# Halving the relu blocks, scoring three bursts ahead and accumulating in open PSUM banks in a fused attention and MoE kernel

## The chip, the cores and the metric

The kernel runs on one core of a Trainium2 chip. The metric is the device time of one execution in microseconds (us), as the median of several executions on the same chip. Times are compared only with runs of the kernel before that were taken in the same rounds on the same chip.

## The reference, cut to what matters

```python
B, N, m, C = (4, 12544, 32, 128)          # x: B x N x C, inducing: m x C
def mab(q, kv):                            # attention with one head
    s = scale * (q @ kv.transpose(0, 2, 1))
    s = s - s.max(-1, keepdims=True)
    a = np.exp(s)
    a /= a.sum(-1, keepdims=True) + 1e-09
    return a @ kv
h = mab(I, x)                              # phase 1: 32 inducing points look at a batch's 12544 tokens
attn_out = mab(x, h)                       # phase 2: every token looks at the 32 rows of h
# MoE, d_ff = 1024
h1 = x @ w1 ; h2 = x @ w2                  # x is attn_out now
out = np.maximum(h1, h2) @ w_out
```

The kernel uses max(a, b) = b' + relu(a - b), folds h into the weights (hwd = h times (w2 - w1), m1 = h times w1 times w_out), and never forms attn_out. What is left per 128 tokens in phase 2 is: relu of (hwd with e2), then w_out, plus the m1 part, divided by the softmax's sum.

## The kernel before

A batch has 98 columns of 128 tokens. Phase 1 gives h; phase 2 goes through **blocks** of 16 columns (a few smaller ones at the ends). A block's **stage** computes scores and exponentials e2. A **burst** is a set of matmuls in four row groups that fills four PSUM banks; ScalarE (ACT) and VectorE (DVE) empty them through a relu into SBUF. A **final** is the 16 matmuls of two columns' relu with w_out; every second one is led by one matmul of e2 with m1. Finals wait in a queue and one is taken after each burst. Phase 1 of the next batch (transposes of x by DMA into xT, scores, exponentials, sums) is woven in between.

```python
relup = ctx.enter_context(tc.tile_pool(name="relup", bufs=2))
# ... phase 1, sums of batch 0, after each tile of exponentials:
            if b == 0:
                # ...
                nc.vector.reduce_sum(
                    out=st[b]["esum"][:, i, :] if i < NP1 - 1 else st[b]["pre"][:, 1, :],
                    in_=et[:, 0:n, :].rearrange("p k m -> p m k"),
                    axis=mybir.AxisListType.X,
                )
# ... the loop of phase 2:
            for blk in all_blocks[b]:
                for u in range(blk.nburst):
                    blk.burst(u)                       # 4 matmuls of 32x512 (block of 16)
                    if u == min(2, blk.nburst - 1) and id(blk) in nxt:
                        nxt[id(blk)].stage()
                    # ...
                    if queue:
                        blk_p, *a = queue.pop(0)
                        blk_p.final(*a)
                    if u == 0:
                        blk.dens()
                    for f, *a in jobs.pop(s, ()):      # phase 1 of the next batch
                        f(*a)
                    # ... after the last burst of the block: queue += blk.finals()
```

The last block of a batch has two columns and one burst, so the first block of the next batch was staged one burst ahead.

The softmax here doesn't subtract the row's maximum and nothing guards it: scores larger than these inputs give would overflow.

## Time and profile before

| | before |
|---|---|
| median, range | 366.03 us, 365.21 to 369.34 (3 runs) |
| profiled execution | 363.5 us, granted clock 0.980 |
| PE, PEld, DVE, ACT busy | 93%, 69%, 79%, 79% |
| longest waits of PE | x loads 5.5 us in 5 waits, e2 (ACT) 4.3 us in 5, xT (DMA) 2.6 us in 2 |

The shares hide stages with different limits, so I read this kernel by bursts. The start of each of the 196 bursts (49 per batch) is in the trace; burst 0 is the first of all, 49, 98 and 147 open the other batches, 195 is the last. The lines that carry the reading are in the prediction below.

### The profile page before, as it was taken

The numbers are of one execution on the slowest core, as the hardware profiler recorded it, in microseconds if no ns is written. First come the engines' busy times: TensorE is split into PE (matmuls) and PEld (weight loads), VectorE is DVE, ScalarE is ACT, GpSimd is POOL, SyncE is SP. The second block draws the span as 40 slices with busy tenths as digits, with TensorE's granted clock in tenths as the row PEclk, the third lists the DMA queues.
The fourth block names the chain that finished last, engine by engine and source line by source line (L and its number), as shares of the span: only waits on it lengthen the run. The fifth ranks groups of instructions, "written<-read, shape, count | busy, mean of one in ns | idle before, by whom it ended". The sixth has DMA issues, their size and how long they took to land.

```text
span 363.5 us, 12262 instructions
## 1 busy us (share of the span) xinstructions
PE 339.8 (93%) x5303; PEld 252.4 (69%) x5303; DVE 286.1 (79%) x520; ACT 287.4 (79%) x550; POOL 96.3 (26%) x166
## 2 busy tenths in 40 slices
PE   7776799999999999999999799999998999999994
PEld 3564457777766777777766577777776777777784
DVE  2456897888899788878998587888898888888871
ACT  2544797898888988888989579898988989999950
POOL 6060111344521223443211124232211212211112
PEclk9997898999999999999999899999999999999999
DMA  7999549969923994997225995122221213222232
GB/s 121 246 188 213 136 110 184 220 145 201 248 103 95 194 224 140 195 215 209 89 85 80 211 211 138 74 76 88 89 88 60 92 70 118 90 87 88 91 117 101
DMA packets 51637, 50.28 MB, mean 138 GB/s; under 512 B 41440, under 2 KB 41984, under 8 KB 51584
## 3 DMA queue, kind: packets, MB, share of 16 engines
q0 software_dynamic: 13232, 39.85, 40.5%
q1 hardware_dynamic: 38352, 9.65, 17.6%
q8 instruction: 41, 0.67, 0.8%
q14 instruction: 12, 0.10, 0.1%
HBM read 27.28 MB, written 25.69 MB: 146 GB/s over the span
## 4 chain that ended last, share of the span: by engine, by line
PE 36%; issue 34%; POOL 9%; DMA 3%; ACT 3%; DVE 2%; POOLq 0%
PE ps L443 20%; PE ps L398 8%; POOL out_dram L460 7%; PE ps L432 4%; DMA xT<-xn 3%; ACT relu L417 2%; POOL eacc L253 2%; PE ps L191 2%; PE ps L213 1%; DVE relu L413 1%; DVE o L453 1%; PE ps L342 1%; ACT hwd L301 0%; ACT e L352 0%; PE ps L363 0%
## 5 line engine op out<-in xcount | busy, mean ns | idle before, releaser
L417 ACT ACTIVATE relu<-ps 128x512 f16<-128x512 f32 x479 | 254.1, 602 | 36.1 <-PE ps L398 34.8
L413 DVE TENSOR_SCALAR relu<-ps 128x512 f16<-128x512 f32 x305 | 199.1, 684 | 39.2 <-PE ps L398 37.3
L443 PE MATMUL ps<-woutp,relu 128*128 128x128 f16 x3136 | 210.2, 221 | 0.0
L443 PEld LDWEIGHTS <-relu 128*128 128x128 f16 x3136 | 186.4, 99 | 33.1 <-issue 21.5
L460 POOL DMA_DIRECT2D out_dram<-o x100 | 54.4, 544 | 249.0 <-DVE o L453 172.9
L398 PE MATMUL ps<-e,hwd 32*128 32x512 f16 (+2 forms) x896 | 81.2, 363 | 5.4 <-ACT e L352 4.3
L453 DVE TENSOR_TENSOR o<-ps,rp 128x512 f32<-128x512 f32 (+1 forms) x100 | 67.2, 672 | 7.1 <-PE ps L443 6.3
L398 PEld LDWEIGHTS <-hwd 32*128 32x128 f16 x896 | 22.3, 93 | 24.1 <-issue 7.8
L432 PE MATMUL ps<-m,e 128*128 128x512 f16 (+1 forms) x100 | 38.8, 388 | 0.3
L432 PEld LDWEIGHTS <-e 128*128 128x128 f16 x100 | 9.6, 96 | 21.6 <-issue 21.2
L200 ACT ACTIVATE et<-ps 128x512 f16<-128x512 f32 (+1 forms) x28 | 15.5, 553 | 6.9 <-PE ps L191 5.9
L352 ACT ACTIVATE e<-ps 128x512 f16<-128x512 f32 (+2 forms) x30 | 16.5, 549 | 3.1 <-PE ps L342 3.1
L253 POOL TENSOR_TENSOR eacc<-eacc,et 128x512 f32<-128x512 f32 (+1 forms) x18 | 18.5, 1028 | 0.2
L183 ACT COPY xT<-ps 128x1024 f16<-128x1024 f16 x6 | 6.1, 1012 | 15.0 <-PE ps L175 15.0
L191 PE MATMUL ps<-inducingT,xT 128*128 128x32 f16 x392 | 14.1, 177 | 2.6 <-DMA xT<-xn 2.6
L107 POOL DMA_DIRECT2D xn<-in_x_dram x28 | 15.5, 561 | 1.5 <-POOLq L600 0.8
L191 PEld LDWEIGHTS <-xT 128*128 128x128 f16 x392 | 12.6, 96 | 3.1 <-issue 3.1
L213 PE MATMUL ps<-et,xn 128*128 128x32 f16 x392 | 14.2, 177 | 0.4 <-ACT et L200 0.4
L213 PEld LDWEIGHTS <-xn 128*128 128x128 f16 x392 | 12.6, 96 | 0.5 <-issue 0.5
L175 PE MATMUL ps<-identity,xn 128*128 128x128 f16 x98 | 6.7, 219 | 5.8 <-DMA xn<-in_x_dram 5.5
L342 PE MATMUL ps<-xT,hT 128*32 128x512 f16 (+2 forms) x120 | 11.1, 359 | 0.8 <-DVE hT L282 0.8
L175 PEld LDWEIGHTS <-xn 128*128 128x128 f16 x98 | 5.6, 98 | 8.5 <-DMA xn<-in_x_dram 7.9
(54 smaller groups left out, 90.7 us busy)
## 6 DMA issues: line engine op xcount, KB each, us to landing
out_dram<-o POOLq DMA_DIRECT2D x96, 256.0 KB, 2.6
xn<-in_x_dram POOLq DMA_DIRECT2D x24, 512.0 KB, 8.3
wf<-in_moe_w_dram POOLq DMA_DIRECT2D x2, 512.0 KB, 14.6
out_dram<-o POOLq DMA_DIRECT2D x4, 128.0 KB, 3.1
xT<-xn SPq DMA_TRANSPOSE x21, 6.4
xn<-in_x_dram POOLq DMA_DIRECT2D x4, 64.0 KB, 10.9
woutp<-in_moe_w_out_dram POOLq DMA_DIRECT2D x1, 256.0 KB, 15.1
ind_sb<-in_inducing_dram SPq DMA_DIRECT2D x1, 16.0 KB, 1.6
```

The source lines that it names most:

```text
L107: nc.gpsimd.dma_start(out=xn_of(b, i)[:, 0:n, :], in_=xr[b, :, k0 : k0 + n, :])
L191: nc.tensor.matmul(out=ps[:, j * M : (j + 1) * M], lhsT=xT_tiles[b % 2][:, k0 + j, :], rhs=inducingT, start=True, stop=True,)
L213: nc.tensor.matmul(out=ps[:, 0:M], lhsT=xn[:, j, :], rhs=et[:, j, :], start=(j == 0), stop=(j == n - 1),)
L253: nc.gpsimd.tensor_add(out=acc, in0=acc, in1=et[:, 0:n, :])
L352: nc.scalar.activation(out=self.e2[:, 0 : self.width], in_=ps[:, 0 : self.width], func=AF.Exp, scale=scale,)
L398: nc.tensor.matmul(out=ps[:, jj * w : (jj + 1) * w], lhsT=st[self.b]["hwd"][32 * q : 32 * (q + 1), 128 * jb : 128 * (jb + 1)], rhs=self.e2 ...
L413: nc.vector.tensor_scalar(out=dst, in0=src, scalar1=0.0, scalar2=None, op0=ALU.max)
L417: nc.scalar.activation(out=dst, in_=src, func=AF.Relu)
L432: nc.tensor.matmul(out=ps[:, 0 : 128 * g], lhsT=self.e2[:, 128 * f : 128 * (f + 1)], rhs=st[self.b]["m1"][:, 0:g, :], start=True, stop=False,)
L443: nc.tensor.matmul(out=ps[:, 128 * q : 128 * (q + 1)], lhsT=self.relu[:, jb, f, q, :], rhs=woutp[:, jb, :], start=False, stop=(q == g - 1 ...
L453: nc.vector.tensor_mul(osb[:, 0:g, :], ps[:, 0 : 128 * g].rearrange("p (q c) -> p q c", q=g), self.rp[:, f, 0:g, :].broadcast_to((128, g, ...
L460: nc.gpsimd.dma_start(out=outr[self.b, :, k : k + g, :], in_=osb[:, 0:g, :])
```

## The change

It has four parts. (1) A block of 16 is worked on in two halves of 256 columns, each with a relu buffer of its own (three buffers of half the size), so that a block's finals enter the queue after four bursts instead of eight. (2) Every block is staged three bursts ahead, also across batches. (3) In batch 0 the sums of exponentials and h are accumulated in two PSUM banks that stay open through the phase; the last loads are split, the order of the weights' preparation is changed, and hwd of batch 0 is made in quarters. (4) m1 takes one masked multiply instead of four copies. For (2) the next batch's h must be there earlier: its steps come three bursts earlier in each batch (from burst 41 instead of 44), and the phase-1 scores of batch 1 come every 4 bursts instead of every 4.5.

```diff
-    relup = ctx.enter_context(tc.tile_pool(name="relup", bufs=2))
+    relup = ctx.enter_context(tc.tile_pool(name="relup", bufs=3))
...
+        step = 8 if i == NP1 - 2 else n
+        units += [(i, g, min(step, n - g)) for g in range(0, n, step)]
...
+        def u_accum(i):
...
+            for name in ("h", "sum"):
+                ps = pool0[name][1]
+                for j in range(n):
+                    nc.tensor.matmul(
+                        out=ps[:, 0:M],
+                        lhsT=xn[:, g + j, :] if name == "h" else ones16,
+                        rhs=et[:, j, :],
+                        start=(i == 0 and j == 0),
+                        stop=(i == NU - 1 and j == n - 1),
+                    )
...
-            for q in range(4):
-                r = slice(32 * q, 32 * (q + 1))
-                nc.vector.tensor_copy(out=m1[r, q, :], in_=ps[r, 0:128])
+            nc.vector.tensor_mul(
+                m1,
+                ps[:, None, 0:128].broadcast_to((128, 4, 128)),
+                mask.broadcast_to((128, 4, 128)),
+            )
...
+                tn = min(2, self.t)
+                self.parts = [Part(self, t0, tn) for t0 in range(0, self.t, tn)]
...
+        stages = {}
+        for blk in flat:
+            stages.setdefault(max(-1, first[blk.name] - 3), []).append(blk)
...
+        for g, (p, u) in enumerate(seq):
+            p.burst(u)
+            for blk in stages.get(g, ()):
+                blk.stage()
...
+            if u == p.nburst - 1:
+                queue += p.finals()
```

## The prediction

> **What bounds the kernel now.** I read the busy time by stretch first, cut at the first burst of each batch (a burst is the four-row-group matmul of hwd with e2 that fills four PSUM banks; a final is the 16 matmuls of relu with w_out that follow), then the timeline of the stretches that stood out, then the waits.
>
> ```profile
> 32.12:44.86 12.74, 9.93 (x156) 7.06 (x156) 9.55 (x21) 9.02 (x20) 1.10 (x2) 0.75 0.73 151
> 44.86:58.41 13.55, 12.98 (x151) 8.07 (x150) 11.54 (x20) 12.02 (x24) 1.25 (x3) 0.89 0.68 140
> ...
> 194.27:277.98 83.71, 80.42 (x1271) 60.51 (x1271) 69.01 (x124) 69.47 (x134) 20.55 (x33) 0.98 0.48 117
> 277.98:349.37 71.39, 71.39 (x1048) 51.98 (x1047) 61.39 (x103) 64.99 (x125) 12.96 (x24) 1.00 0.24 88
> 349.37:363.50 14.13, 9.22 (x158) 8.56 (x150) 4.66 (x9) 1.57 (x3) 3.24 (x6) 0.97 0.27 103
> ```
>
> The columns are stretch, length, then busy us of PE, PEld, DVE, ACT, POOL, then the granted clock. The last batch (fifth line shown) has PE busy all through: 71.39 us for 49 bursts, 1.457 us each, with ACT at 91% and DVE at 86%. The early stretches (first two) run at clock 0.75 and 0.89 with DVE and ACT nearly full instead, and in the last 14 us ACT works 1.57 us. So the bound changes, and the steady part is PE's own sequence:
>
> ```profile
> 309.34 0.39 PE L398 MATMUL ps<-e,hwd 32*128 32x512 f16 x4
> ...
> 309.67 1.07 PE L443 MATMUL ps<-woutp,relu 128*128 128x128 f16 x16
> ...
> 310.67 0.39 PE L398 MATMUL ps<-e,hwd 32*128 32x512 f16 x4
> ...
> 311.00 0.39 PE L432 MATMUL ps<-m,e 128*128 128x512 f16 x1
> ...
> 311.22 1.06 PE L443 MATMUL ps<-woutp,relu 128*128 128x128 f16 x16
> ```
>
> Start to start: burst 0.33, final 1.00, burst 0.33, m1 matmul plus final 1.21: 2.87 us for two bursts, no gap. After the last burst (349.04) only finals are left:
>
> ```profile
> 351.63 1.95 PE L443 MATMUL ps<-woutp,relu 128*128 128x128 f16 x32
> ...
> 353.63 1.95 PE L443 MATMUL ps<-woutp,relu 128*128 128x128 f16 x32
> ...
> 355.63 1.95 PE L443 MATMUL ps<-woutp,relu 128*128 128x128 f16 x32
> ```
>
> Each pair of finals with its m1 matmul takes 2.00 us, with ACT idle. At each change of batch PE waits for the first block's exponentials, because its scores are issued one burst ahead:
>
> ```profile
> 193.55 0.67 ACT L352 ACTIVATE e<-ps 128x512 f16<-128x512 f32 x1
> ...
> 194.27 0.40 PE L398 MATMUL ps<-e,hwd 32*128 32x512 f16 x4 [0.69 <-ACT e L352]
> ```
>
> The bracket is idle time and who ended it: 0.69 us here, 0.78 at 114.31 and 0.69 at 277.98.
>
> **What the Trainium skill says.** "Perfetto Trace Analysis", Identifying the Most-Contended Engine: matmul occupancy is no measure of closeness to roofline; interleaving regimes with different limits can help. The trace agrees on both: PE reads 100% with PEld at 73% in the last batch, and the finals-only tail stands beside an early stretch with few finals. "TensorE: Matmul & The Clock Gate", Part 1: an idle PE is throttled and must earn the clock back over about 3.4 us. This trace: at 56.41, after four bursts without finals (51.3 to 55), 15 matmuls of a final took 1.81 us against 1.07 for 16; the page slice at 30 to 40 us was granted 0.66. "PSUM — Partial Sum Buffer", The four PSUM rules: a first matmul clears the accumulate bits of its whole bank, so two open groups need separate banks, as the change does; no run yet shows it. "VectorE: DVE Perf Modes" gives a PSUM-source op a fixed part (120 cycles) plus its length: four small m1 copies pay it four times. The trace agrees: the four 32x128 copies took 1.18 us at 192.13, a 128x512 multiply 0.68.
>
> **The change part by part.**
>
> *Start.* The last big x block arrives at 23.02. Today's chain from there to the first burst at 32.12 is 9.1 us: transposes, copies, w1T transposes (26.08 to 27.15) in the way, three DVE reductions (1.00+0.48+0.21), two float sums through PE (29.39), reciprocal 0.36, h 0.29, hwd evictions 0.69, burst. Now the block comes in two pieces, w1T goes before them (its weights are in by 20.75), and DVE's reductions become 98 ones-matmuls of 32 columns. Those go at 0.51/16 = 32 ns, so PE does 16 more (0.5 us) per block. Following PE's order I get (estimate): w1T to 21.9; transposes, scores and sums through 25.85; the last pieces' scores, exps and sums done at 27.7; reciprocal and h 28.5; scores 28.7; hwd in quarters, DVE two at about 0.4 each, 29.7; first burst 29.8. Gain 2.3 us.
>
> *First 16 bursts.* Before, burst 0 to 7 took 12.74 us with 9.55 us of DVE work. w1out now precedes them, m1 is one 0.68 us multiply instead of four copies, scores of the first two blocks are ready. I take ACT and DVE as the bound: 10.0 us. Bursts 7 to 16 took 13.55 us with five finals and then a slow clock; halves let a block's finals start after four bursts instead of eight, so nine finals run: 9 x 1.435 = 12.9, plus 1.0 for a stage, denominators and the first scores of batch 1 = 13.9. Burst 16 then starts at 29.8+10.0+13.9 = 53.7 instead of 58.41: gain 4.7 in all (2.3 of it above), and four finals are already done.
>
> *Bursts.* A half is 256 wide, so 184 bursts (23 blocks of 16, eight each) need 8 matmuls instead of 4; the instruction order shows 1632 instead of 896. The 8-wide block in today's trace has this form: burst 42.32, next PE work 42.65, 0.33, the same as for 512 wide. Cost 0. ACT evicts 476 instead of 479 and DVE 308 instead of 305 banks: nothing.
>
> *Changes of batch.* Scores three bursts ahead remove 0.69+0.78+0.69 = 2.2 us of PE wait; DVE also loses 0.5 us per m1. But ACT and DVE are backlogged there (six relus in a row before the exponentials), so I count 0.6 each: 1.8 us.
>
> *Tail.* The last queue is four finals shorter: two pairs at 2.00 = 4.0 us. PE does them in the early part, where they are paid for above.
>
> Sum 4.7 + 1.8 + 4.0 = 10.5 us; I keep 1.0 back for waits that move. 366.0 - 9.5 = 356.5 us.
>
> **The rivals.** (1) *Doubled burst matmuls cost PE.* Speaking for it: 736 more weight loads of 91 ns. At 0.05 us a burst, 184 bursts lose 9 us and the result is 366. Against: the 0.33 us above. (2) *Half boundaries stall.* A half's first final comes one burst after its last eviction was ordered, now 48 times instead of half as often, and ACT runs up to 1.6 us behind. At 0.1 us each, 2 to 3 us: 359. Against: at today's boundaries the final shows idle 0.0. (3) *ACT and DVE are the real bound* (91% and 86%). Then only tail and start pay: about 359. (4) *The transposing DMA takes the gain.* In batch 2 PE waits 2.31 us for xT at 204.13, and then runs slow until 208; its trigger sits behind an output in POOL's order, unchanged by the edit, so I let this loss stay. In batch 1 the transposes were due at about 115.35 + 6.4 = 121.75 and PE came at 121.9: if PE comes sooner, a new wait plus slow clock of up to 2.5 us makes 359.
>
> **Range and chances.** Tail 4.0 is the surest. The early gain could be 2.5 to 6, the batch changes 0.5 to 2.5, rivals 2 to 4 could take 0 to 4. That gives 353 to 360.5. 2% is 358.7, so gains under 7.3 us count as the same: faster 0.79, same 0.20, slower 0.01.
>
> **What would show it.** First burst near 29.8, burst 16 near 53.7 without a clock dip at 50 to 60; a burst of 8 matmuls followed by PE work after 0.33; PE busy throughout the last batch at about 1.46 us per burst; no wait of the burst for exponentials at the three changes; about 5 us of finals after the last burst instead of 9. Wrong if the last batch lengthens (rivals 1 to 3), if a wait for xT grows or a second one appears (4), or if the first burst is later than 31.

## The result

The changed kernel took **355.73 us** (median of 4 runs, 354.4 to 356.72); the kernel before took 365.62 us in the same rounds (4 runs, 364.49 to 369.34). The ratio is 0.971, 95% interval 0.9631 to 0.9789: faster. (A ratio here is the mean time of one kernel's fast runs over the mean of the other's fast runs of the same rounds, so it is not quite the ratio of the quoted medians.) The spans of the profiled executions went from 363.5 to 354.5 us.

Busy time by stretch of the changed kernel, cut at bursts 0, 7, 16, then 98, 147, 195 and the end. The columns are as in the prediction: stretch, length, busy us of PE, PEld, DVE, ACT, POOL (with counts), granted clock, mean share of the DMA engines, GB/s.

```profile
29.37:39.90 10.53, 9.15 (x144) 6.37 (x144) 7.57 (x16) 7.83 (x18) 0.56 (x1) 0.84 1.06 213
39.90:54.77 14.87, 14.54 (x254) 10.76 (x249) 13.37 (x23) 13.82 (x27) 2.89 (x6) 1.00 0.80 140
189.26:272.84 83.58, 80.31 (x1466) 61.04 (x1464) 68.49 (x121) 69.69 (x137) 20.62 (x34) 0.98 0.43 118
272.84:344.03 71.19, 71.19 (x1227) 52.65 (x1225) 61.72 (x105) 65.43 (x127) 13.32 (x25) 1.00 0.23 93
344.03:354.46 10.43, 5.54 (x102) 5.02 (x100) 3.60 (x7) 1.76 (x4) 2.17 (x4) 0.93 0.23 90
```

The first burst starts at 29.37 instead of 32.12 us. The fourth line, the last batch, is still wholly PE: 71.19 us, so its 191 more matmuls (1227 recorded, against 1036 with whole blocks, below) cost it next to nothing. The last line is the tail: 10.43 us where it was 14.46. The third line is the disappointment: batch 2 takes 83.58 us, of which PE works 80.31, as long as before.

The timeline of PE, in the last batch and behind the last burst:

```profile
336.79 0.40 PE L455 MATMUL ps<-e,hwd 32*128 32x256 f16 x8
337.12 1.07 PE L498 MATMUL ps<-woutp,relu 128*128 128x128 f16 x16
338.12 0.40 PE L455 MATMUL ps<-e,hwd 32*128 32x256 f16 x8
338.44 0.39 PE L487 MATMUL ps<-m,e 128*128 128x512 f16 x1
...
346.62 1.95 PE L498 MATMUL ps<-woutp,relu 128*128 128x128 f16 x32
348.41 0.27 PE L487 MATMUL ps<-m,e 128*128 128x256 f16 x1
348.52 1.06 PE L498 MATMUL ps<-woutp,relu 128*128 128x128 f16 x16
```

A burst of 8 matmuls of 256 columns is followed by PE's next work after 0.33 us (336.79 to 337.12), as the burst of 4 matmuls of 512 was. Once the pair at the last burst is done, one more pair and a single final are left, where there were three pairs and a single one. At the change of batch and in the middle of batch 2:

```profile
189.16 0.17 PE L412 MATMUL ps<-ones,e 128*128 128x4 f16 x1
189.26 0.43 PE L455 MATMUL ps<-e,hwd 32*128 32x256 f16 x8
...
199.41 0.59 PE L262 MATMUL ps<-inducingT,xT 128*128 128x32 f16 x16 [2.79 <-DMA xT<-xn]
199.94 0.61 PE L455 MATMUL ps<-e,hwd 32*128 32x256 f16 x8
200.48 0.62 PE L391 MATMUL ps<-xT,hT 128*32 128x512 f16 x4
201.03 1.85 PE L498 MATMUL ps<-woutp,relu 128*128 128x128 f16 x16
```

The first burst of the batch no longer waits for e2 (no bracket). But the wait for xT stands, 2.79 us, and the final after it takes 1.85 us instead of 1.06: from 199.41 to 203.00 us the granted clock was 0.54.

Where the 9.04 us between the two profiled spans lie (the lengths are differences of burst starts in the two traces):

| stretch | before | after | gain |
|---|---|---|---|
| start to burst 0 | 32.12 | 29.37 | 2.75 |
| 0 to 7 | 12.74 | 10.53 | 2.21 |
| 7 to 16 | 13.48 | 14.87 | -1.39 |
| 16 to 49 | 55.97 | 55.04 | 0.93 |
| batch 1 (49 to 98) | 79.96 | 79.45 | 0.51 |
| batch 2 (98 to 147) | 83.71 | 83.58 | 0.13 |
| batch 3 (147 to 195) | 71.06 | 71.19 | -0.13 |
| tail | 14.46 | 10.43 | 4.03 |

Part of this is the granted clock. In the kernel before it was 0.75, 0.90 and 0.98 in bursts 0 to 7, 7 to 16 and batch 2, in the changed kernel 0.84, 1.00 and 0.98. Length times the share not granted gives 6.2 us lost before and 3.4 us after (an estimate), so some 3 of the 9 us are a clock that PE kept.

### The profile page after: what moved, and what is told of

The parts are those of the page before. It is cut to its first block, busy times and chain, and to the rows that moved or that the text cites. A ratio compares the mean times of both kernels' runs of the same rounds, so it can differ in the third digit from the quotient of the medians.

```text
span 354.5 us, 13957 instructions
## 1 busy us (share of the span) xinstructions
PE 338.7 (96%) x6131; PEld 256.1 (72%) x6131; DVE 280.1 (79%) x497; ACT 286.4 (81%) x549; POOL 96.9 (27%) x167
## 4 chain that ended last, share of the span: by engine, by line
issue 41%; PE 30%; POOL 12%; DMA 2%; DVE 1%; ACT 1%; POOLq 0%
PE ps L498 17%; POOL out_dram L515 8%; PE ps L455 6%; PE ps L487 3%; POOL eacc L304 3%; DMA xT<-xn 2%; PE ps L391 1%; PE ps L262 1%; POOL xn L114 1%; PE ps L284 1%; ACT relu L474 1%; DVE o L508 1%; DVE relu L470 0%; POOL eacc L301 0%; DVE esum L309 0%
## 5 line engine op out<-in xcount | busy, mean ns | idle before, releaser
L455 PE MATMUL ps<-e,hwd 32*128 32x256 f16 (+1 forms) x1632 | 81.0, 271 | 1.6 <-issue 0.8
L455 PEld LDWEIGHTS <-hwd 32*128 32x128 f16 x1632 | 25.8, 92 | 19.5 <-issue 4.0
L271 ACT ACTIVATE et<-ps 128x512 f16<-128x512 f32 (+1 forms) x21 | 11.5, 546 | 8.1 <-PE ps L262 7.8
L197 DVE COPY xT<-ps 128x1024 f16<-128x1024 f16 (+1 forms) x7 | 4.4, 634 | 13.8 <-PE ps L192 13.8
L262 PE MATMUL ps<-inducingT,xT 128*128 128x32 f16 x294 | 10.6, 177 | 2.8 <-DMA xT<-xn 2.8
L114 POOL DMA_DIRECT2D xn<-in_x_dram x21 | 11.5, 555 | 0.6 <-POOL xn L137 0.6
L262 PEld LDWEIGHTS <-xT 128*128 128x128 f16 x294 | 9.5, 96 | 2.9 <-issue 2.9
L284 PE MATMUL ps<-et,xn 128*128 128x32 f16 x294 | 10.6, 176 | 0.0
L174 PE MATMUL ps<-warm 128*128 128x512 f16 x26 | 8.7, 460 | 1.2 <-DVE warm L158 1.2
L421 DVE RECIPROCAL rp<-ps 128x16 f32<-128x16 f32 (+2 forms) x30 | 7.2, 239 | 3.3 <-PE ps L412 1.4
```

The lines of the kernel that those rows point to most:

```text
L114: nc.gpsimd.dma_start(out=xn_of(b, i)[:, 0:n, :], in_=xr[b, :, k0 : k0 + n, :])
L262: nc.tensor.matmul(out=ps[:, j * M : (j + 1) * M], lhsT=xT_tiles[b % 2][:, k0 + j, :], rhs=inducingT, start=True, stop=True,)
L455: nc.tensor.matmul(out=ps[:, jj * w : (jj + 1) * w], lhsT=st[blk.b]["hwd"][r, 128 * jb : 128 * (jb + 1)], rhs=blk.e2[r, 128 * self.t0 : 12 ...
```

## The experiments

Twelve kernels ran, all with five rounds, all correct. Each call had its own runs of the kernel before, so kernels are compared by ratio across calls and by time within one.

### First call: repeat, whole blocks, scores as before, later phase-1 scores

Kernel before: 366.05 us (median of 11). The theory at this point: the halves are worth most of the gain, the early scores about 2 us, and a PE wait for xT in batch 2 eats part of it. The rival: doubled burst matmuls cost PE, so halves give little.

**ctl**: the changed kernel, unedited.

> The changed kernel again, as the base of this set: span 354.5 us, time 355.7 us, ratio to the kernel before 0.971. First burst at 29.4, burst 16 at 54.8, last burst at 344.0, one wait for xT of 2.8 us near 199.

Measured: 355.31 us, ratio 0.9697 [0.9654, 0.974]. Its profiled execution was an outlier of 1018 us, and its trace is not used. The five others took 352.62 to 355.97 us. The result repeats.

**whole**: blocks in one piece again, the rest of the change kept.

```diff
-                tn = min(2, self.t)
+                tn = self.t
-    relup = ctx.enter_context(tc.tile_pool(name="relup", bufs=3))
+    relup = ctx.enter_context(tc.tile_pool(name="relup", bufs=2))
...
-                        [128, NJB, self.tn, blk.g, 128], F16, name=f"relu_{self.name}", tag="relu"
+                        [128, NJB, self.tn, blk.g, 128], F16, name=f"relu_{self.name}",
+                        tag="relu" if blk.n > 4 else "relu_small"
```

> The changed kernel with whole blocks again (relu tiles of a whole block, bursts of four 512-wide matmuls). Theory (halves only move four finals from the tail to the early bursts): after the last burst 14.1 us instead of 10.5, the clock dips again between 45 and 55, and the time is 3 to 4.5 us longer, about 359.5. Rival (the doubled burst matmuls, or the boundaries of halves met twice as often, cost PE time): the last batch gets shorter than 71.2 us by 1 us or more, and the time rises by under 2 us.

Measured: 354.07 us (353.35 to 354.54), ratio 0.9678 [0.9647, 0.971]. My expectation missed: without halves the kernel is as fast as with them. Its stretches 7 to 16, batch 2, batch 3 and tail:

```profile
39.26:52.30 13.04, 12.57 (x152) 7.29 (x146) 12.56 (x22) 12.44 (x26) 1.80 (x4) 1.00 0.76 163
186.78:266.57 79.79, 79.09 (x1274) 59.32 (x1271) 69.00 (x122) 69.30 (x135) 20.56 (x34) 1.00 0.52 123
266.57:337.65 71.08, 71.08 (x1036) 51.79 (x1034) 61.55 (x105) 65.44 (x126) 13.27 (x25) 1.00 0.23 92
337.65:352.05 14.40, 9.54 (x168) 8.78 (x166) 4.98 (x9) 1.75 (x4) 3.24 (x6) 1.00 0.26 102
```

The tail is back at 14.40 us, as it should be. But batch 2 takes 79.79 us instead of 83.58: PE did not wait for xT at all in it. The loss of the tail was paid by a gain that has nothing evident to do with blocks. Batch 3, 71.08 us against 71.19, says that the doubled matmuls of the halves cost PE 0.1 us per batch, so that rival fell here.

**stage1**: the scores placed as before (third burst of the block before, or its last one).

```diff
-            stages.setdefault(max(-1, first[blk.name] - 3), []).append(blk)
+            g = -1 if prev is None else first[prev.name] + min(2, nb - 1)
+            stages.setdefault(g, []).append(blk)
```

(nb is the number of bursts of the block before, prev.)

> The changed kernel with a block's scores issued where they were before (after the third burst of the block ahead, so one burst ahead at a change of batch). Theory (three bursts ahead removes a PE wait of 0.7 us at each change, of which the wait for xT in batch 2 takes one back): waits for the exponentials return, about 0.7 us each, the wait for xT in batch 2 falls from 2.8 to about 2.3, and the time is 1 to 2 us longer, about 357. Rival (ACT and DVE are the bound at the changes of batch, so the wait only moves): under 0.5 us.

Measured: 357.79 us (354.09 to 359.5), ratio 0.9758 [0.9708, 0.9809], which is "unclear" by the 2% verdict; 2.5 us over the repeat by medians, though the ranges and the intervals overlap. Two lines of its waits (us in total, times, longest):

```profile
PE ps L455 <- ACT e L401: 4.9, 6, 1.2
...
PE ps L262 <- DMA xT<-xn: 1.6, 1, 1.6
```

The six waits of a burst for exponentials are back, 4.9 us; in the changed kernel this line is absent. Three of them lie in bursts 0 to 7 (3.26 us), three at the changes of batch (0.32 + 0.64 + 0.64 = 1.60 us). So the early scores take these waits away. What they gain in time is not settled: the profiled execution was the fastest of the six (354.09 us), and its span of 352.1 us is shorter than the changed kernel's.

**late**: in the phase 1 of batches 2 and 3, each tile's scores and accumulation come two bursts later.

```diff
-                s = g + (14 + 4 * i if b == 0 else 4 + 5 * i)
+                s = g + (14 + 4 * i if b == 0 else 6 + 5 * i)
```

> The changed kernel with the scores and sums of batches 2 and 3 two bursts later. Theory (the 2.8 us wait for xT near 199 and the slow clock after it are a loss of their own on the path): no wait for xT, no clock dip near 200, the time 3 to 4 us shorter, about 352. Rival (the work then collides later, or the sums come too late for the next h at burst 42): the time changes by under 1 us, with a wait for the sums at the ends of batches 1 and 2.

Measured: 350.55 us (350.23 to 351.67), ratio 0.9581 [0.9547, 0.9615]: 4.8 us faster than the repeat by medians. Its one wait for xT is 0.3 us and batch 2 takes 79.84 us.

```profile
PE ps L262 <- DMA xT<-xn: 0.3, 1, 0.3
```

So the wait for xT costs the changed kernel about 3.7 us (83.58 to 79.84): 2.79 of wait, and the rest goes with the slow clock behind it. The two profiled spans differ by more, 4.89 us: another 1.72 lies in bursts 0 to 7, which took 10.53 us at a clock of 0.84 in the changed kernel and 8.81 at 1.00 here. That is ahead of all that this edit moves, so it is not the edit's doing. And with the wait away in both, halves against whole blocks are 350.55 against 354.07 us: **the halves are worth some 3.5 us**, as first thought. (Only one of the two has the later scores. A pair without them, in the second call, gives 3.2 us: shift, 350.94, against last2, 354.12, where all blocks but one are whole.) What remained open is why whole blocks had no wait to begin with.

### Why some kernels wait for xT

The first transpose for the next batch is asked for at the change of batch, and PE comes for its result some five bursts later. In the traces of this call and of the two kernels it took either 3.9 to 4.7 us or 5.7 to 7.3 us. The packets of the trace show a second thing: one DMA queue (q8, kind "instruction") carries packets of 16,384 bytes, 41 before, 48 after, 42 with whole blocks. PE has 10,606, 12,262 and 10,790 instructions in these traces (matmuls and weight loads), so one packet is 256 of PE's instructions. Where such a packet falls among the transposes, single packets of these, 0.018 us in the median, take 1 to 2 us. The changed kernel's packet comes at 193.22 us, and the transpose asked for at 192.70 takes 6.58 us. With whole blocks the packets are at 186.14 and 197.41 us, outside the transpose asked for at 190.16, which takes 3.91 us. The theory: halves add 1,472 PE instructions, which shifts where the packets fall; the wait is a matter of where one lands. The rival: chance, or the moment of asking.

### Second call: moving the packets, halves at the end only, sums by VectorE

Kernel before: 368.19 us (median of 11).

**shift**: the changed kernel with its 18 warm-up matmuls at the start made narrower and more numerous: 108 instructions more, no other edit.

```diff
-        keep_warm(18)
+        bi, ps = bank([128, 512])
+        for _ in range(72):
+            nc.tensor.matmul(out=ps[:, 0:128], lhsT=warm[:, 0:128], rhs=warm[:, 0:128], start=True, stop=True)
+            end = model.pe(128 / 2400, model.bank_free[bi])
+        model.bank_free[bi] = end
```

> The changed kernel with its first 18 warm-up matmuls of 512 columns written as 72 of 128 columns: the same columns, 54 more matmuls and 54 more weight loads, so 108 more TensorE instructions ahead of everything else. In the traces so far TensorE's instructions came in packets of 16,384 bytes, one for each 256 instructions, and the first transpose of x for batch 3 (asked for at 192.70 us) took 6.58 us with such a packet at 193.22 us, but 3.91 us where none fell inside it. Theory: the packets move some 2 to 3 us earlier against the work, to about 190 to 191 us, the first transpose lands within 4.5 us, the wait for xT of batch 2 falls from 2.8 us to 0.5 us or less, the stretch from burst 98 to burst 147 from 83.59 to about 80 us, and the time from 355.3 to about 351.8 us. Rival (the transposes' time is chance, or is set by the halves themselves): no change, 355 us, the wait stays at 1.5 us or more.

Measured: 350.94 us (350.44 to 352.97), ratio 0.9555 [0.9512, 0.9599]. The packet is at 189.76 us, the transpose asked for at 191.20 took 3.80 us, there is no wait for xT, batch 2 takes 79.55 us. The packet came slightly earlier than forecast (190 to 191 us); the rest is as the theory had it. (Other packets now fell on the first transposes for batches 1 and 2, which took 6.03 and 5.32 us; PE waited for neither.) The first burst is where it was, 29.36 us. Here is the bandwidth of all DMA in 40 slices of 0.2 us, first the changed kernel from 192 to 200 us, then this one from 190.5 to 198.5 us:

```profile
GB/s 0 0 0 0 0 266 512 307 225 3 142 252 211 60 0 20 0 41 6 18 200 288 289 296 292 289 360 571 328 328 533 223 283 276 65 81 285 296 288 289
```
```profile
GB/s 0 0 0 0 0 287 410 348 266 2 195 288 289 292 291 292 289 288 288 262 278 268 282 253 246 207 180 221 239 108 288 118 52 38 320 312 76 265 400 258
```

The first non-zero slices of each are an output's transfer; the transposes follow in slice 10, some 1.3 us after they were asked for, in both. In the second line they run on at about 290 GB/s. In the first they all but stop for seven slices, 194.6 to 196.0 us; the stop begins as the instruction packet (193.22 us, 1.53 us long) ends. It makes 1.4 of the 2.78 us between the two transposes' times; the rest is not visible as a pause. Why a packet stops them, no trace shows.

**whole_hit**: whole blocks, with the warm-up made 134 instructions longer, to put a packet onto the transpose.

```diff
-        keep_warm(18)
+        for _ in range(85):
+            nc.tensor.matmul(out=ps[:, 0:108], lhsT=warm[:, 0:128], rhs=warm[:, 0:108], start=True, stop=True)
```

> The kernel with whole blocks, with its 18 warm-up matmuls of 512 columns written as 85 of 108 columns: 134 more TensorE instructions, which move the packet that was at 197.41 us with whole blocks to about 191 to 192 us, just behind the first transpose of x for batch 3 (asked for at 190.16 us). Theory: that transpose takes about 6 us instead of 3.91 us, the wait for xT in batch 2 comes back (1.5 to 3 us, against none), the stretch from burst 98 to burst 147 grows from 79.79 to 82 us or more, and the time from 354.07 to about 356.5 us. Rival (whole blocks escape the wait because they ask for the transposes at another moment, not because of the packets): no change, 354 us.

Measured: 355.3 us (353.16 to 357.78), ratio 0.967 [0.9621, 0.9719]. The packet missed the place I aimed at: it came at 190.24 us, in front of the transpose asked for at 190.92, which took 4.06 us; batch 2 did not change (79.77 us). By accident another one came with the first transpose for batch 2, at 108.75 us where that was asked for at 108.80: it took 6.52 us instead of 4.49 with whole blocks, and PE waited 1.3 us for it (the other wait, 0.36 us, is in batch 2).

```profile
PE ps L262 <- DMA xT<-xn: 1.6, 2, 1.3
```

Batch 1 became 80.79 us instead of 79.35. So the forecast was wrong on the place; the effect, in another batch, is the theory's. In time it is within the noise of the ratios.

**last2**: whole blocks everywhere, but the last block of 16 of the last batch in halves that share the block's one buffer.

```diff
-                tn = min(2, self.t)
+                tn = 2 if b == B - 1 and k0 == K - 18 else self.t
...
+                    if self.t0 == 0:
+                        blk.relu = relup.tile([128, NJB, blk.t, blk.g, 128], F16, ...)
+                    self.relu = blk.relu[:, :, self.t0 : self.t0 + self.tn]
```

> Whole blocks everywhere except the last block of 16 of the last batch, which is done in halves (that share the block's one relu tile, so no buffer more). Theory: the halves pay at the end of the kernel only (tail 14.4 us with whole blocks, 10.4 us with halves), and cost 1.8 us in bursts 7 to 16; so this takes 4 us off the time with whole blocks: 354.07 becomes about 350 us, with the tail at 10.4 us and bursts 7 to 16 at 13.0 us. Rival (halves need their own buffers, or help in the middle of the batches): 352 us or more.

Measured: 354.12 us (352.96 to 354.88), ratio 0.9631 [0.9593, 0.967]. My expectation missed: the tail is 14.40 us, exactly that of whole blocks, and after its last burst PE runs the same finals.

```profile
337.73:352.13 14.40, 9.54 (x168) 8.78 (x166) 4.99 (x9) 1.75 (x4) 3.24 (x6) 0.92 0.25 101
```

The reason is in the queue. One final is taken per burst, so a half that is done early at the end only stands behind the finals of the block before. Counting finals (16 matmuls of relu with w_out) between bursts in the traces shows it:

| finals in stretch | 0 to 7 | 7 to 16 | 16 to 40 | 40 to 49 | batch 1 | batch 2 | batch 3 | tail |
|---|---|---|---|---|---|---|---|---|
| before, whole, last2 | 3 | 5 | 24 | 9 | 49 | 49 | 48 | 9 |
| after, shift | 3 | 9 | 24 | 9 | 49 | 49 | 48 | 5 |
| quarters (below) | 5 | 9 | 24 | 9 | 49 | 49 | 48 | 3 |

All have 196. Halves move four finals from the tail to bursts 7 to 16, and this happens at the front of the kernel, once. The tail does not shorten because the last block is halved, but because the queue has been four finals shorter since burst 16.

**dvesum**: the sums of batch 0 by VectorE and two fp32 matmuls, as before; h stays in its open bank.

```diff
-            for name in ("h", "sum"):
+            for name in ("h",):
...
+            nc.vector.reduce_sum(
+                out=pool0["es"][:, i, :] if i < NU - 1 else pool0["pre"][:, 1, :],
+                in_=et[:, 0:n, :].rearrange("p k m -> p m k"),
+                axis=mybir.AxisListType.X,
+            )
```

> The changed kernel with the sums of batch 0 made as before: VectorE reduces each tile of exponentials, and two fp32 matmuls with ones add up over the partitions, in place of the open PSUM bank of ones matmuls; h stays in its open bank. Theory: the end of phase 1 of batch 0 waits again for the last VectorE reduction and the fp32 matmuls, so the first burst comes 1 to 1.5 us later than in the changed kernel (29.4 us), at about 30.6 us, and the time is about 356.5 us. Rival (the start gained by the smaller last loads alone): first burst at 29.4 us, 355.3 us.

Measured: 352.96 us (352.09 to 355.83), ratio 0.9616 [0.9571, 0.9662]. The wait of the theory is there, though half as long as I thought:

```profile
27.30 0.60 PE L261 MATMUL ps<-esum_pre,ones 128*128 128x32 f32 x4 [0.88 <-DVE esum_pre L244]
```

The first burst is at 29.91 us, 0.54 later than in the changed kernel, not 1 to 1.5. The time did not rise to 356.5 but fell below the changed kernel's. The edit also took PE instructions away ahead of the transposes: the packet came at 191.07 us, the transpose asked for at 192.31 took 3.88 us, and batch 2 took 79.62 us. Another packet, at 113.92 us, now fell inside the first transpose for batch 2: that took 5.88 us, and PE waited 0.63 us for it in batch 1. An edit for one purpose moved the packets for another.

### Third call: a whole packet's shift, the kernel before, quarters, no split load

Kernel before: 367.55 us (median of 11).

**shift256**: as in shift, but with 256 instructions more, one packet's worth (146 warm-up matmuls of 63 columns).

> The changed kernel with its 18 warm-up matmuls of 512 columns written as 146 of 63 columns (on 64 rows of output), so 256 more TensorE instructions ahead of everything else: one packet's worth exactly, where the run with 108 more had made the wait vanish. Theory (each 16,384-byte packet of TensorE's instructions slows the transposes that it falls on): the packets come back to the places of the changed kernel, one of them inside the first transposes for batch 3; that transpose takes 5.7 us or more again, TensorE waits 1.5 us or more for xT in batch 2, the stretch from burst 98 to burst 147 is back at 82 us or more, and the time at about 355. Rival (narrow warm-up matmuls help by themselves): as with 108 more, no wait, about 79.6 us and 351 us.

Measured: 355.47 us (353.42 to 358.33), ratio 0.9701 [0.9649, 0.9754]: the changed kernel's ratio in its repeat was 0.9697. The packet is back, at 193.06 us, within the transpose asked for at 192.62. In the profiled execution, a fast one of 351.4 us, the transpose took 4.88 us, the wait was 1.08 us and batch 2 80.63 us, all short of the 5.7, 1.5 and 82 us that I had put down. The time is as expected, and the rival (narrow warm-up matmuls help by themselves) is out: 108 more instructions took the ratio to 0.9555, 256 more bring it back. The profiled execution, the fastest of the six, shows where only part of this comes from: batch 2 is 1.08 us longer than in shift, and bursts 0 to 7 are 0.98 us longer (9.79 us at a clock of 0.83). Why the clock fell in those first bursts is open.

**before_shift**: the kernel before with 140 more warm-up instructions (88 matmuls of 104 columns).

> The kernel before with its 18 warm-up matmuls of 512 columns written as 88 of 104 columns: 140 more TensorE instructions, which should move the packets at 119.62 and 199.54 us (inside the first transposes for batches 2 and 3) some 4 to 5 us earlier, in front of both. Theory: the first transpose for batch 3 takes 4.5 us instead of 6.29 us, the wait for xT in batch 2 falls from 2.3 to 0.5 us or less, the stretch from burst 98 to burst 147 from 83.71 to about 81 us, and the time from 366 to about 363 us. Rival: no change.

Measured: 365.56 us (363.56 to 366.56), ratio 0.9955 [0.9907, 1.0002], not told apart from no change by the time. In the profile the transpose for batch 3 took 4.47 us instead of 6.29, the longest wait for xT was 0.5 us, and batch 2 took 80.52 us instead of 83.71. Against this stands the start of this execution: PE waited 3.10 us for x at 23.34 us, its clock fell, and the first burst came at 34.64 us.

```profile
23.34 1.89 PE L175 MATMUL ps<-identity,xn 128*128 128x128 f16 x16 [3.10 <-DMA xn<-in_x_dram]
```

So the kernel before had the same loss in batch 2, 3.2 us of it removable; whether the later start is the edit's doing stays open.

**quarter_late**: the changed kernel in quarters of a block. (The name is wrong: the later scores of the run "late" were not in it.)

```diff
-                tn = min(2, self.t)
+                tn = min(1, self.t)
-    relup = ctx.enter_context(tc.tile_pool(name="relup", bufs=3))
+    relup = ctx.enter_context(tc.tile_pool(name="relup", bufs=6))
```

> The changed kernel with quarters of a block (parts one 128-column group wide, six relu buffers). A block's finals can then start after two bursts instead of four. Theory, as corrected by the run with halves in the last block only: the smaller parts do no less work, they move two more finals from the tail to bursts 7 to 16, where TensorE has waits to fill; so tail 8.4 us instead of 10.4 us, bursts 7 to 16 about 0.9 us longer (15.8), bursts of 16 matmuls at no cost: about 1 us faster than the changed kernel with the same xT wait (about 354.3 us with a wait of 2.8 us, 350 us without). Rival (bursts of 16 matmuls cost TensorE): the last batch's 71.19 us between bursts 147 and 195 grows by 1 us or more.

Measured: 356.48 us (354.05 to 361.94), ratio 0.9701 [0.9648, 0.9754], no faster than halves. The tail is 8.40 us, as expected to the digit:

```profile
345.32:353.72 8.40, 3.54 (x69) 3.13 (x67) 2.92 (x6) 1.76 (x4) 1.62 (x3) 0.99 0.20 80
```

The last batch is 71.43 us, 0.24 more than with halves (but nounits, with halves, has 71.43 too), so bursts of 16 matmuls cost PE little. The 2 us went elsewhere: bursts 16 to 40 took 42.75 us instead of 40.06, batch 1 81.30 us instead of 79.45. Two gaps in the former, 1.14 and 0.98 us, and one of 0.87 us in batch 1 lie inside bursts, and the profile names no wait for them:

```profile
55.55 0.23 PE L455 MATMUL ps<-e,hwd 32*128 32x128 f16 x2 [1.14 <-issue]
```

PE has 15,270 instructions here in 59 packets, and a packet comes 2 us ahead of this gap while the transposes run. That PE had run out of instructions is a guess that no run tested. It is not the quarters' alone: the changed kernel and whole have such a gap in an early burst, 0.79 and 0.72 us.

**nounits**: the next to last tile of batch 0 loaded and worked on in one piece.

```diff
-        step = 8 if i == NP1 - 2 else n
+        step = n
-    W_AT = NU - 3
+    W_AT = NU - 2
```

> The changed kernel with the next to last tile of x of batch 0 loaded and worked on in one piece of 16 again instead of two of 8. Theory: of the 2.75 us by which the first burst moved, the two pieces are worth about 1 us; first burst at about 30.4 us instead of 29.4 us, time 1 us longer than the changed kernel's with the same xT wait. Rival (the order of the weights' transposes and the ones matmuls give all of it): first burst at 29.4 us.

Measured: 355.67 us (354.71 to 357.11), ratio 0.9696 [0.9651, 0.9741]. The first burst is at 30.01 us, 0.64 later than in the changed kernel; I had expected 1. In time that is not to be told apart. The eight kernels that share the rest of this start (the changed one, whole, late, shift, whole_hit, last2, shift256, quarters) had it between 28.79 and 29.59 us, so 0.64 and the 0.54 of dvesum are just outside that spread. The packet at 193.11 us was inside the transpose (6.37 us) and the wait was 2.6 us.

### All packets together

First transpose for batch 3 in each kernel: when asked for, the packet nearest to it, how long it took, the wait of PE for xT in batch 2, and the length of batch 2. "Ahead" and "inside" go by the start of the packet. (The medians are from different calls.)

| kernel | asked at | packet at | took | wait | batch 2 | median |
|---|---|---|---|---|---|---|
| before | 197.71 | 199.54, inside | 6.29 | 2.31 | 83.71 | 365.62 |
| after | 192.70 | 193.22, inside | 6.58 | 2.79 | 83.58 | 355.73 |
| nounits | 192.27 | 193.11, inside | 6.37 | 2.58 | 82.12 | 355.67 |
| stage1 | 192.44 | 193.28, inside | 5.70 | 1.6 | 81.51 | 357.79 |
| shift256 | 192.62 | 193.06, inside | 4.88 | 1.08 | 80.63 | 355.47 |
| late | 191.58 | 193.14, inside | 7.29 | 0.30 | 79.84 | 350.55 |
| quarters | 196.53 | 195.96, ahead | 4.86 | 1.07 | 80.83 | 356.48 |
| shift | 191.20 | 189.76, ahead | 3.80 | none | 79.55 | 350.94 |
| dvesum | 192.31 | 191.07, ahead | 3.88 | none | 79.62 | 352.96 |
| whole_hit | 190.92 | 190.24, ahead | 4.06 | 0.36 | 79.77 | 355.30 |
| last2 | 190.41 | none near | 3.91 | none | 79.62 | 354.12 |
| whole | 190.16 | none near | 3.91 | none | 79.79 | 354.07 |
| before_shift | 201.97 | none near | 4.47 | 0.50 | 80.52 | 365.56 |

With a packet starting inside it, the transpose took 4.88 to 7.29 us; with none, 3.80 to 4.86 us. The first transposes for batches 1 and 2 of the same 13 traces say the same: 5.32 to 6.50 us with a packet inside (4 of them), 3.95 to 4.70 without (19); of three with a packet up to 0.1 us before the asking, two took 6.03 and 6.52 us and one 4.36, so a packet does not always slow one. Single packets of transposes took over 1 us in 91 places of these traces; 89 of the places begin between 0.3 us before and 2 us after the start of an instruction packet, though such a packet comes only every 7 us or so. That speaks against chance, the first half of the rival. Against the second, the moment of asking, speak shift and late: asked for at 191.20 and 191.58 us, the transpose took 3.80 us without a packet inside and 7.29 us with one.

The two ways out of the wait, moving the packet (shift) and coming later for the result (late), give the same time within their intervals (ratios to before 0.9555 and 0.9581), and both beat the changed kernel (0.9697). Of the two, **late** is the one to keep: in its trace the transpose took 7.29 us and PE waited only 0.30, while shift depends on every edit ahead of it.

## Why the prediction was right

The predicted time, 356.5 us, and the range, 353 to 360.5, hold: 355.73 us. In this there is some luck. The same program with its instruction packets elsewhere (shift) takes 350.94 us, below the range, and no step of the prediction had looked at them. Its steps one by one:

- **Start**, 2.3 us: 2.75 in the trace. Two of its causes measured apart: the ones matmuls in an open bank 0.54 us, the split of the last tile 0.64 us, each at the edge of the scatter. The rest (order of the weights, hwd in quarters, copies) was not taken apart.
- **Bursts 0 to 7**, 10.0 us: 10.53 us, but at a clock of 0.84, and with the gap of 0.79 us of which the profile names no cause. At full clock they took 8.81 us (late, shift, dvesum, nounits, last2, whole_hit), so the term was too large by 1.2 and the slow clock hid it. The prediction had expected no clock dip only for 50 to 60 us, and there was none there; it did not count one in the very first bursts.
- **Bursts 7 to 16**, 13.9 us with nine finals: nine finals as counted, but 14.87 us, also at full clock. PE's own work was sized rightly: stage1 and the quarters, where burst 7 takes its usual time, have 13.92 and 13.97 us. In the changed kernel burst 7 takes 1.28 us instead of 0.33, because PE waits in it for banks that DVE and ACT still empty:

```profile
39.68 0.98 PE L455 MATMUL ps<-e,hwd 32*128 32x256 f16 x8 [0.26 <-DVE o L508]
40.88 0.37 PE L455 MATMUL ps<-e,hwd 32*128 32x256 f16 x5 [0.23 <-ACT relu L474]
```

  So the bound by ACT and DVE, which the prediction put into bursts 0 to 7, reaches one burst further. This is why the sum fits at full clock: 23.9 us predicted for bursts 0 to 16, 23.69 measured. With the dip it was 25.41, and burst 16 came at 54.77 us instead of 53.7.
- **Bursts of 8 matmuls cost nothing**: right; 0.33 us to PE's next work, 71.19 against 71.08 us in the last batch (halves against whole). Rivals 1 and 2 are out, and so is rival 3 in this stretch, where PE has no gap; at burst 7 it holds.
- **Changes of batch**, 1.8 us: the waits for exponentials went, and came back when the scores were put back (stage1), 1.6 us of them at the changes of batch. Of the 1.8 the two traces show 0.93 + 0.51 + 0.13 - 0.13 = 1.44 us over bursts 16 to 195, almost none of it in batch 2, where the wait for xT grew from 2.31 to 2.79 us. With little or no such wait on either side (before_shift against shift) the same bursts take 287.37 and 285.45 us: 1.9 us, of which 0.50 is a wait for xT left in before_shift.
- **Tail**, 4.0 us: 4.03. And the note that PE does these finals in the early part is what the count of finals shows.
- **Rival 4**, the transposing DMA: the loss in batch 2 stayed, as the prediction let it, 2.79 us where it was 2.31. Its second half, a new wait in batch 1, did not come in the changed kernel; it came in whole_hit (1.3 us) and dvesum (0.63 us), each time with a packet in the transpose. What failed is the reason given for the loss to stay (the trigger's place behind an output in POOL's order): it stays or goes with a packet of instructions, which no step of the prediction had looked at.

The 1.0 us held back for "waits that move" stands for what was lost by the terms above: 10.5 without it, 9.04 by the spans, 9.9 by the medians. Three readings of the prediction are to be put right: DVE and ACT were not "nearly full" in bursts 0 to 7 (9.55 and 9.02 of 12.74 us); burst 16 of the kernel before came at 58.34 us, not 58.41; and its last stretch ends after the last burst, so bursts there start every 1.48 us (71.06 us for 48), not 1.457. The advice to interleave regimes, too, stands in the page's section Optimization Strategy, not in the one named. My first reading after the result, that halves bring 3 to 4.5 us, looked refuted by whole and was not: with the wait out of both it is 3.2 to 3.5 us. The tail gives 3.99 us (14.40 less 10.41) and bursts 0 to 16 take back 0.6 to 0.8 (23.69 in late against 23.08 in last2 and 22.92 in whole_hit). These two ran bursts 7 to 16 at clocks of 0.90 and 0.88, late at 1.00; no trace of whole blocks has bursts 0 to 16 at full clock, where the halves would take back more.

## What to carry to other kernels

Ask where the work goes that a change takes out of a tail: halving the blocks took no final away but moved four of them to where PE still had waits, and halving only the last block moved none. When undoing one part of a change makes up for what it should cost, look for a second effect before calling the part useless; here it was 256 instructions per packet, and the count of instructions ahead of a transfer decided 4 us of batch 2 (83.58 us in the changed kernel, 79.55 in shift). Put the consumer of a transfer far enough behind it that its slow case is covered too: two bursts were enough.

## What the Trainium skill lacked or had wrong

- "Runtime: NRT & Kernel Launch", Instruction fetch mechanics, says that an engine's instructions are refilled in blocks of 16 KiB (256 instructions) over a DMA queue of its own, and that crossing a block's boundary is "mostly hidden". The traces agree with the size (48 packets of 16,384 bytes for PE's 12,262 instructions). They don't agree with "hidden" where such a packet meets DMA transposes: the first transpose for batch 3 took 4.88 to 7.29 us with one starting inside and 3.80 to 4.86 us without, and moving the packet by 108 instructions took the ratio to the kernel before from 0.9697 to 0.9555.
- "DMA: Bandwidth & Descriptors", DMA Transpose (X-bar), has nothing on what other DMA traffic does to a transpose's duration. In these runs packets of a transpose that take 0.018 us in the median took over 1 us in 91 places, 89 of them beside an instruction packet.
- The same section of "Runtime: NRT & Kernel Launch" says that fetching is hidden, as instructions are dispatched more slowly than they are fetched. The quarters (15,270 PE instructions) have gaps of 1.14, 0.98 and 0.87 us inside bursts that no wait explains. Whether PE starved for instructions there is not settled by any run.
